# Attention with hash buckets and a routed expert: products with 128 rows, 16-byte places for V, signs as bits and complements

## The chip, the core and the metric

The kernel runs on one core of one Trainium2 chip, in one launch. The metric is the time of one execution in microseconds. Three runs of the kernel before took 401.94, 402.27 and 403.64 us; the median is 402.27 us.

## The reference, cut to what matters

```python
# q, k, v: (B=4, H=8, S=768, D=64) float32; proj: (64, 6)
bits(x)  = (x @ proj > 0)                       # 6 bits per token
mask     = bucket(q)[:, None] == bucket(k)[None, :]
scores   = where(mask, q @ k.T / 8, -1e9);  scores -= max(scores)
attn     = exp(scores) / (sum + 1e-9);      x = attn @ v      # 32 heads
# then, per batch b, x is (768, 512):
s        = x @ w_gate;  top = the 128 tokens with the largest s
out      = x;  out[top] += sigmoid(s[top]) * (relu(x[top] @ w1) @ w2)
```

## The kernel before, in words

The 32 heads go through one software pipeline. For each head there are two tiles in SBUF of 16-bit numbers. Tile A (97 partitions) holds q and k, split to their high parts, in rows 32 to 95, and sign rows for the hash above them: rows 0 to 5 are the centred signs of q and k (plus or minus 2^13), and row 6 is a constant row (2^13 for q, -6 * 2^13 for k), so that a product over these rows is 0 where all six signs agree and very negative elsewhere. Row 96 has -2^12 on k's side and, on q's side, the row's maximum divided by 2^12, which a later step puts there. Tile B (128 partitions) holds the low parts that correct the product. The region of A between q and k (tile K) has the difference of k's two halves.

Four kinds of product fill TensorE. `max_unit` (line 645) multiplies rows 0 to 95 of A, 384 columns at a time, twice for each of six row blocks: once with the difference of the halves, once with the second half. ScalarE takes the positive part of the one (`max_relu`, line 653), VectorE adds the other and keeps the maximum (`max_red`, line 662). When all six maxima of a head are there, TensorE turns them (`max_turn`), ScalarE copies them (`max_copy`), and SyncE's queue sends them as a row into A (`max_row`). `st_unit` then forms the scores minus the maximum, transposed: a product with 97 rows of A (line 693) and one with 128 rows of B (line 697) into the same PSUM bank, with 512 or 256 columns. ScalarE takes the exponential (`st_exp`, lines 711 and 713); VectorE or GpSimd splits it into a 16-bit high part, which is read in place, and a low part R (`r_chunk`, lines 728 and 731). `av` (line 755) multiplies these with V, in groups of three for each block of 128 by 128: high part with V's high part (65 columns: 64 and the sum), high part with V's low part (64 columns), low part with V's high part (65 columns). Each call of `av` does three such groups. `recip` and `norm` divide.

V sits in SBUF as [128, 6 blocks, 2 heads, 131 numbers of 2 bytes]: one number for the gate's score, 64 of V's high part, one for the sum, then the low part. Thirty-one heads skip the first number, so the high part that is read starts 2 bytes, and the low part 134 bytes, behind a multiple of 262 bytes.

Signs of all heads but the first come from `hash_half` (fp32 products, line 472) and `signs` (lines 489 to 496, VectorE): compare with zero, subtract the halves, subtract 2^13. Two DMAs for each head place them (`place_signs`). The first head has steps of its own at the start: `init_first` loads q and k, `hash_first` hashes them, `sign_first` (line 402) and `centre_first` (line 414) make the signs, `diff_first` (line 420) the difference. `init_crow` and `init_a` write the constant row with GpSimd, and `init_row` row 96. `keep_warm` issues products of ones that nobody reads.

The order of all this is written out by hand: `ORDER` lists 2698 steps, and each engine's queue, SyncE's DMAs too, gets its instructions in that order. Nothing is reordered after that.

Of the kernel before, what the change touches and what calls it, by code (L numbers as in the profile page):

```python
# [20 lines left out]
P = 128  # L21
NC = S // P
# [6 lines left out]
SG = 2.0 ** 13  # L29
MS = 2.0 ** 12  # L30
# [5 lines left out]
VC = 2 * D + 3  # L36
# [13 lines left out]
PJW = 66  # L50
ORDER = (
# [189 lines left out]
def body(ctx, tc, qk, v, pj, wg, w1, w2, cst, out):  # L241
# [348 lines left out]
    def sum_v(pr):  # L590
# [5 lines left out]
        if not o0:  # L596
            need("gvl")
# [730 lines left out]
```

## Time and profile before

| | |
|---|---|
| median of three runs | 402.27 us |
| profiled execution | 401.58 us |
| its span, first to last instruction | 399.8 us |
| TensorE busy | 387.0 us, 97% of the span |
| VectorE busy | 336.9 us, 84% |
| ScalarE busy | 332.8 us, 83% |
| GpSimd busy | 184.5 us, 46% |
| mean granted TensorE clock | 0.995 |

The prediction is worked out against the profiled execution, which spent 1.8 us outside its span. A product on TensorE overlaps the next one, so the duration of one in a row is longer than its share of the engine; what one product costs is read from the start of one row to the start of the next. `PE` is TensorE, `PEld` its loads of the stationary operand, `DVE` VectorE, `ACT` ScalarE, `POOL` GpSimd.

### The profile page before, as it was taken

The numbers are of one execution on the slowest core, as the hardware profiler recorded it, in microseconds if no ns is written. First come the engines' busy times: TensorE is split into PE (matmuls) and PEld (weight loads), VectorE is DVE, ScalarE is ACT, GpSimd is POOL, SyncE is SP. The second block draws the span as 40 slices with busy tenths as digits, with TensorE's granted clock in tenths as the row PEclk, the third lists the DMA queues.
The fourth block names the chain that finished last, engine by engine and source line by source line (L and its number), as shares of the span: only waits on it lengthen the run. The fifth ranks groups of instructions, "written<-read, shape, count | busy, mean of one in ns | idle before, by whom it ended". The sixth has DMA issues, their size and how long they took to land.

```text
span 399.8 us, 14395 instructions
## 1 busy us (share of the span) xinstructions
PE 387.0 (97%) x5770; PEld 278.3 (70%) x5770; DVE 336.9 (84%) x929; ACT 332.8 (83%) x818; POOL 184.5 (46%) x107
## 2 busy tenths in 40 slices
PE   5899999999999998999999999999999999999995
PEld 4356677677667776678567777677677778687794
DVE  4989898889999988987999798989999979769733
ACT  6779999999999998997769999999898997775310
POOL 7526576665756446345233444363525270520112
PEclk9989999999999999999999999999999999999999
DMA  6558655766665555546265636565163526100211
GB/s 221 134 164 233 191 157 170 212 163 175 186 222 132 146 177 154 173 118 181 74 184 161 147 91 172 154 200 171 42 162 93 139 44 170 24 21 2 105 32 53
DMA packets 25619, 55.44 MB, mean 139 GB/s; under 512 B 3850, under 2 KB 10582, under 8 KB 25552
## 3 DMA queue, kind: packets, MB, share of 16 engines
q1 hardware_dynamic: 15104, 35.97, 34.5%
q10 hardware_dynamic: 9680, 16.45, 12.5%
q0 software_dynamic: 768, 2.11, 1.7%
q8 instruction: 45, 0.74, 0.8%
q14 instruction: 22, 0.18, 0.2%
HBM read 26.19 MB, written 7.35 MB: 84 GB/s over the span
## 4 chain that ended last, share of the span: by engine, by line
PE 83%; issue 9%; DMA 2%; POOL 2%; ACT 2%; DVE 1%; POOLq 0%; SPq 0%; DVEq 0%; ACTq 0%
PE av L755 24%; PE st L693 15%; PE bank L645 15%; PE st L697 15%; PE bank L472 3%; PE bank L973 3%; PE bank L997 2%; DMA A<-mr 2%; PE av L740 1%; PE wq L303 1%; PE bank L601 1%; DMA Xa<-in_qk_dram 1%; ACT me L653 1%; POOL R L731 1%; DVE R L728 1%
## 5 line engine op out<-in xcount | busy, mean ns | idle before, releaser
L731 POOL TENSOR_TENSOR R<-P 128x1536 f16<-128x1536 f32 x46 | 135.9, 2957 | 153.4 <-ACT P L711 31.9
L755 PEld LDWEIGHTS <-P 128*128 128x128 bf16 x2304 | 129.0, 97 | 29.1 <-issue 1.0
L755 PE MATMUL av<-V,P 128*128 128x65 f16 (+2 forms) x2304 | 136.9, 194 | 0.0
L755 PE MATMUL av<-V,R 128*128 128x65 f16 (+1 forms) x1152 | 129.6, 193 | 0.8 <-DVE R L728 0.8
L711 ACT ACTIVATE P<-st 128x512 f32<-128x512 f32 x192 | 113.9, 608 | 14.9 <-PE st L697 8.9
L693 PE MATMUL st<-A 97*128 97x256 f16 (+1 forms) x384 | 120.7, 329 | 0.7 <-DMA A<-mr 0.5
L662 DVE CUSTOM_DVE_ANT_0 mj<-bank,me 128x384 bf16<-128x384 f32 x192 | 102.4, 553 | 21.6 <-ACT me L653 9.4
L697 PE MATMUL st<-B 128*128 128x256 f16 (+1 forms) x384 | 120.5, 328 | 0.0
L645 PE MATMUL bank<-A 96*128 96x384 f16 x384 | 107.6, 327 | 1.8 <-DVE M L662 0.7
L755 PEld LDWEIGHTS <-R 128*128 128x128 f16 x1152 | 107.5, 99 | 1.0 <-DVE R L728 1.0
L653 ACT ACTIVATE me<-bank 128x384 f32<-128x384 f32 x192 | 93.8, 503 | 12.2 <-PE bank L645 5.6
L728 DVE TENSOR_TENSOR R<-P 128x768 f16<-128x768 f32 x100 | 94.6, 966 | 1.2 <-ACT P L713 1.0
L713 ACT ACTIVATE P<-st 128x512 f32<-128x512 f32 x96 | 58.1, 609 | 1.3 <-PE st L697 1.3
L693 PEld LDWEIGHTS <-A 97*128 97x128 f16 x384 | 37.7, 98 | 17.4 <-issue 2.6
L697 PEld LDWEIGHTS <-B 128*128 128x128 f16 x384 | 37.8, 99 | 15.2 <-issue 0.9
L645 PEld LDWEIGHTS <-A 96*128 96x128 f16 x384 | 34.7, 98 | 19.2 <-issue 2.7
L779 ACT ACTIVATE x<-av,rc 128x64 f32<-128x64 f32 x192 | 44.1, 331 | 0.5 <-DVE rc L767 0.4
L509 DVE SCALAR_TENSOR_TENSOR T<-X,T 128x768 f16<-128x768 f32 x32 | 35.2, 1102 | 0.5 <-ACT T L502 0.5
L502 ACT ACTIVATE T<-X 128x768 f16<-128x768 f32 x32 | 27.1, 857 | 0.0
L973 PEld LDWEIGHTS <-w1h 128*128 128x128 f16 x256 | 15.8, 98 | 1.9
L816 POOL TENSOR_TENSOR w1l<-W,w1h 128x512 bf16<-128x512 f32 x8 | 12.2, 1522 | 10.0 <-ACT P L711 3.9
L662 DVE DVE_READ_ACCUMULATOR2_ANT M<- 128x1 f16 x192 | 16.4, 86 | 0.0
(138 smaller groups left out, 409.2 us busy)
## 6 DMA issues: line engine op xcount, KB each, us to landing
X<-in_qk_dram SPq DMA_DIRECT2D x32, 384.0 KB
B<-T SPq DMA_DIRECT2D x62, 192.0 KB
A<-T SPq DMA_DIRECT2D x31, 240.0 KB
V<-in_v_dram ACTq DMA_DIRECT2D x16, 384.0 KB
out_dram<-x ACTq DMA_DIRECT2D x6, 768.0 KB
W<-in_w_dram ACTq DMA_DIRECT2D x8, 512.0 KB
sbc<-scores SPq DMA_DIRECT2D x3, 384.0 KB
out_3l_dram<-x ACTq DMA_DIRECT2D x1, 768.0 KB
```

The costliest lines, as they stand in the source:

```text
L509: mine(nc.vector.scalar_tensor_tensor(t[:, o : o + S], st["X", p, r], XS, t[:, i : i + S], op0=ALU.mult, op1=ALU.subtract))
L645: nc.tensor.matmul(pt[:, :384], a[0][0:96, t * P : (t + 1) * P], a[1][0:96, 384:768] if i else K[h % NA][0:96], start=True, stop=True,)
L653: nc.scalar.activation(me, st["mx", h, t, 0][:, :384], AF.Relu)
L662: nc.vector.tensor_tensor_reduce(out=jk, in0=st["mx", h, t, 1][:, :384], in1=st["me", h, t], op0=ALU.add, op1=ALU.max, scale=1.0 / MS, sca ...
L693: nc.tensor.matmul(pt[:, o : o + n], a[1][:, c * P : (c + 1) * P], a[0][:, q0 : q0 + n], start=True, stop=False,)
L697: nc.tensor.matmul(pt[:, o : o + n], bt[:, 0, c * P : (c + 1) * P], bt[:, 1, q0 : q0 + n], start=False, stop=True,)
L711: nc.scalar.activation(pp[:, r, 0:512], pt, AF.Exp, scale=ES)
L713: nc.scalar.activation(pp[:, :, 512:768], pt.rearrange("p (a b) -> p a b", a=2), AF.Exp, scale=ES)
L728: mine(nc.vector.tensor_tensor(t[:, r], pp[:, r], hi_view(pp, r), op=ALU.subtract))
L731: turn(nc.gpsimd.tensor_tensor(t, pp, hi_view(pp, a), op=ALU.subtract))
L755: nc.tensor.matmul(o[:, t, o0:o1], l, vv[:, c, hh, v0 + o0 : v0 + o1], start=False, stop=last and l is lo, skip_group_check=True,)
L779: nc.scalar.activation(x[:, t], o[:, t, 1 : D + 1], AF.Copy, scale=rc[:, t : t + 1])
```

## The change

Four parts.

First, tile A has 128 partitions, and the products of lines 645 and 693 read all of them. GpSimd zeroes rows 96 to 127 at the start (and rows 0 to 31 for three of the four tiles), in `init_a`. The maximum's row moves among the sign rows.

Second, the signs are 0 or a constant, not plus or minus: each of the six bits has a row, and so has its complement, for which the projection is written a second time and `negate` (ScalarE, once) turns it. The compare of `signs` and `sign_first` takes its threshold and its factor from a table with one value for each partition. In that table two further rows come out as constants: the one that was row 6, and the one in which the maximum is put later, which is 0 on q's side until then. So 14 rows are placed for each head, where it was 6, by the same two DMAs. Centring goes: the last instruction of `signs` (line 496), `centre_first`, `init_crow`, `init_row` and the DMAs of the constant row.

Third, V has 144 numbers in the place of 131: V's high part and the sum from 0, the gate's score behind them, the low part from 72. High and low part then start at multiples of 16 bytes. The output columns in PSUM start at 0, no longer at 1.

Fourth, `ORDER` is another list of 2692 steps. Of the steps that both have, half moved by at most 8 places and one in ten by more than 20. At the start, two of the `keep_warm` steps (34 and 8 products) and `negate` stand ahead of `hash_first`; before, 34 stood behind it.

```diff
-VC = 2 * D + 3
+VL = 72
+VC = 2 * VL
-PJW = 66
+PJW = 68
+PF = 27
+QC, KC = 2 * SG, -SG * NB
 ORDER = (
...
-        t = cp.tile([97, KH + S - QH], F16, name=f"A{i}")
+        t = cp.tile([P, KH + S - QH], F16, name=f"A{i}")
...
     def init_a(i):
         st["ia", i] = True
-        e = nc.gpsimd
-        e.memset(AA[i][0:32].bitcast(F32), 0.0)
-        e.dma_start(AA[i][6:7], crow)
+        for p in (0, 96) if i else (96,):
+            nc.gpsimd.memset(AA[i][p : p + 32].bitcast(F32), 0.0)
...
+    def negate():
+        n = 2 * NB + 2
+        x = pjt[:, NB : NB + 3 * n].rearrange("p (j t) -> p j t", t=n)[:, :, :NB]
+        nc.scalar.activation(x, x, AF.Copy, scale=-1.0)
...
         nc.vector.tensor_scalar(
-            sg[:, e * 384 : (e + 1) * 384], hp[r, :384], 0.0, 2 * SG,
+            sg[:, e * 384 : (e + 1) * 384], hp[r, :384], pjt[r, 66:67], pjt[r, 67:68],
             op0=ALU.is_gt, op1=ALU.mult,
         )
         if e:
             nc.vector.tensor_tensor(sd, sg[:, 0:384], sg[:, 384:768], op=ALU.subtract)
-            nc.vector.tensor_scalar(sg, sg, SG, None, op0=ALU.subtract)
...
-        move(a[0:6, KD - QH :], t[j + 32 : j + 38])
-        move(a[0:6, 0:S], t[j : j + 6, S // 2 :])
+        move(a[0:n, KD - QH :], t[j + 32 : j + 32 + n])
+        move(a[0:n, 0:S], t[j : j + n, S // 2 :])
...
         nc.tensor.matmul(
-            pt[:, :384], a[0][0:96, t * P : (t + 1) * P],
-            a[1][0:96, 384:768] if i else K[h % NA][0:96], start=True, stop=True,
+            pt[:, :384], a[0][:, t * P : (t + 1) * P],
+            a[1][:, 384:768] if i else K[h % NA], start=True, stop=True,
         )
...
-        move(A[h % NA][0][96:97], st["mr", h])
+        r = 1 if (h - 1) % 2 else 2 * NB + 1
+        move(A[h % NA][0][r : r + 1], st["mr", h])
...
-        o, o0 = st["O", h], int(h < NH - 1)
+        o, (e, f) = st["O", h], ((OW, OW) if h == NH - 1 else (D + 1, D))
...
-            for l, o1, v0 in ((hi, OW, 0), (hi, D + 1, OW), (lo, OW, 0)):
+            for l, n, v0 in ((hi, e, 0), (hi, f, VL), (lo, e, 0)):
                 nc.tensor.matmul(
-                    o[:, t, o0:o1], l, vv[:, c, hh, v0 + o0 : v0 + o1], start=False,
+                    o[:, t, :n], l, vv[:, c, hh, v0 : v0 + n], start=False,
                     stop=last and l is lo, skip_group_check=True,
                 )
```

## Rows read from the trace of the kernel before

**Rows 1.** The page: busy us of an engine (share of the span), instructions.

```profile
PE 387.0 (97%) x5770; PEld 278.3 (70%) x5770; DVE 336.9 (84%) x929; ACT 332.8 (83%) x818; POOL 184.5 (46%) x107
```

**Rows 2.** Stretches: us, each engine's busy us, PEclk, DMA share, GB/s.

```profile
10.00:20.00 10.00, 8.12 (x55) 3.22 (x52) 9.12 (x25) 7.06 (x13) 5.93 (x18) 1.00 0.54 134
20.00:30.00 10.00, 9.88 (x83) 5.52 (x83) 8.19 (x23) 7.81 (x19) 2.96 (x2) 0.83 0.58 165
30.00:60.00 30.00, 30.00 (x449) 21.15 (x447) 27.12 (x74) 30.00 (x74) 19.69 (x10) 1.00 0.67 193
60.00:100.00 40.00, 40.00 (x623) 28.30 (x622) 35.24 (x94) 39.22 (x102) 24.50 (x11) 1.00 0.64 180
100.00:140.00 40.00, 39.93 (x620) 28.22 (x619) 37.76 (x105) 38.36 (x98) 22.69 (x10) 1.00 0.62 171
...
200.00:240.00 40.00, 40.00 (x659) 28.84 (x658) 35.81 (x105) 35.39 (x91) 16.71 (x7) 1.00 0.54 146
```

**Rows 3.** TensorE's timeline, 192 to 195 us: start, us, line, tiles, shape, count.

```profile
192.22 0.38 PE L997 MATMUL bank<-w2h,hth 128*128 128x512 f16 x1
...
194.16 0.65 PE L645 MATMUL bank<-A 96*128 96x384 f16 x3
```

**Rows 4.** The chain of waits, 66 to 69 us: start, us, what.

```profile
66.26 0.11 PE st L693
...
68.30 0.22 PE st L697
68.52 0.83 PE av L755 x27
```

**Rows 5.** TensorE's timeline, 186 to 188 us.

```profile
186.45 0.22 PE L755 MATMUL av<-V,P 128*128 128x65 f16 x2
...
187.80 0.20 PE L755 MATMUL av<-V,R 128*128 128x65 f16 x1
187.84 0.33 PE L645 MATMUL bank<-A 96*128 96x384 f16 x1
```

**Rows 6.** TensorE's timeline, 262 to 263 us.

```profile
262.43 0.22 PE L755 MATMUL av<-V,P 128*128 128x65 f16 x2
...
262.94 0.19 PE L755 MATMUL av<-V,R 128*128 128x65 f16 x1
262.97 0.22 PE L672 MATMUL bank<-ident,M 128*128 128x128 f16 x1
```

**Rows 7.** TensorE's groups by line and shape: count, busy us, mean ns.

```profile
L755 PE MATMUL av<-V,P 128*128 128x65 f16 x1152 | 129.7, 193 | 0.0
...
L693 PE MATMUL st<-A 97*128 97x512 f16 x192 | 73.6, 383 | 0.5 <-DMA A<-mr 0.5
```

**Rows 8.** All engines' timeline, 0 to 13 us.

```profile
0.75 0.20 POOL L292 MEMSET ones<- 128x128 f16 x1 [0.29 <-POOLq L1308]
...
4.26 1.51 PE L393 MATMUL bank<-Xa,pjt 96*32 96x384 f32 x8 [4.26 <-DMA Xa<-in_qk_dram]
...
5.70 3.81 PE L303 MATMUL wq<-ones 128*128 128x128 f16 x34
...
5.93 1.70 DVE L402 TENSOR_SCALAR A<-bank 7x384 f16<-7x384 f32 x3 [3.42 <-PE bank L393]
...
11.48 1.23 PE L645 MATMUL bank<-A 96*128 96x384 f16 x5
...
12.97 0.56 DVE L662 CUSTOM_DVE_ANT_0 mj<-bank,me 128x384 bf16<-128x384 f32 x1
```

**Rows 9.** VectorE's groups by line: count, busy us, mean ns, idle before.

```profile
L496 DVE TENSOR_SCALAR sg<-sg 128x768 f16<-128x768 f16 (+1 forms) x9 | 3.9, 429 | 0.3
...
L414 DVE TENSOR_SCALAR A<-A,pjt 7x384 f16<-7x384 f16 (+1 forms) x3 | 0.9, 333 | 0.0
```

**Rows 10.** The chain of waits, 140 to 268 us.

```profile
148.61 3.13 DMA A<-mr
...
263.51 2.91 DMA A<-mr
```

More of the change, by code (lines that the diff above doesn't have):

```diff
@@ L29 @@
 SG = 2.0 ** 13
+TH = -(2.0 ** -126)
 MS = 2.0 ** 12
@@ L270, in body @@
     AA, A, Bt, V, K = [], [], [], [], []
-    crow = sb.tile([1, KH + S - QH], F16, tag="x", name="crow", bufs=1)
     for i in range(NA):
-        t = cp.tile([97, KH + S - QH], F16, name=f"A{i}")
+        t = cp.tile([P, KH + S - QH], F16, name=f"A{i}")
         AA.append(t)
@@ L306, in keep_warm @@
         heat(pst.tile([P, 512], F32, tag="st", name=f"wq{i}"), n)
-    def init_row(i):
-        nc.gpsimd.memset(A[i][1][96:97], -MS)
-    def init_crow():
-        for c, a, b in ((SG, 0, S), (0.0, S, KH - QH), (-SG * NB, KH - QH, KH - QH + S)):
-            nc.gpsimd.memset(crow[:, a:b], c)
     def init_a(i):
         st["ia", i] = True
-        e = nc.gpsimd
-        e.memset(AA[i][0:32].bitcast(F32), 0.0)
-        e.dma_start(AA[i][6:7], crow)
+        for p in (0, 96) if i else (96,):
+            nc.gpsimd.memset(AA[i][p : p + 32].bitcast(F32), 0.0)
     def init_rest():
@@ L329, in init_rest @@
         for t in V:
-            nc.gpsimd.memset(t[:, :, :, D + 1 : OW], VS)
-        for x in (0, OW):
-            nc.gpsimd.memset(V[-1][:, :, 0, x : x + 1], 0.0)
+            nc.gpsimd.memset(t[:, :, :, D : D + 1], VS)
+        for x in (D + 1, VL + D, VL + D + 1):
+            nc.gpsimd.memset(V[-1][:, :, :, x : x + 1], 0.0)
     w1h = cp.tile([P, 4, FF], F16, name="w1h")
@@ L393, in hash_first @@
                 nc.tensor.matmul(
-                    hp[j : j + 32, :384], pjt[0:96, 32:64], st["xa"][0:96, r, e * 384 : (e + 1) * 384],
+                    hp[j : j + 32, :384], pjt[0:96, PF : PF + 32], st["xa"][0:96, r, e * 384 : (e + 1) * 384],
                     start=True, stop=True, tile_position=(0, j),
@@ L400, in sign_first @@
         need(("xa", r))
-        j = 32 * (2 * e + r)
+        j, n = 32 * (2 * e + r), 2 * NB + 2
         nc.vector.tensor_scalar(
-            A[0][r][0:7, e * 384 : (e + 1) * 384], st["hpa"][j : j + 7, :384], 0.0, 2 * SG,
-            op0=ALU.is_gt, op1=ALU.mult,
+            A[0][r][0:n, e * 384 : (e + 1) * 384], st["hpa"][j : j + n, :384],
+            pjt[j : j + n, 64:65], pjt[j : j + n, 65:66], op0=ALU.is_gt, op1=ALU.mult,
         )
@@ L408, in sign_first @@
             pmax.give("hpa")
-    def centre_first(r, e):
-        f = slice(0, S) if e is None else slice(e * 384, e * 384 + 384)
-        need(*(("sa", r, x) for x in ((0, 1) if e is None else (e,))))
-        a = A[0][r][0:7, f]
-        nc.vector.tensor_scalar(a, a, pjt[0:7, 64 + r : 65 + r], None, op0=ALU.subtract)
-        st["ca", r, e] = True
     def diff_first():
-        need(("ca", 1, None))
+        need(("sa", 1, 0), ("sa", 1, 1))
         st["ia", 0] = True
@@ L430, in low_first @@
     def low_first(r):
-        need(("xs", r))
-        if r:
-            need(("ca", 1, None))
-        else:
-            need(("ca", 0, 0), ("ca", 0, 1))
+        need(("xs", r), ("sa", r, 0), ("sa", r, 1))
         if "xla" not in st:
@@ L461, in row_first @@
             )
-        nc.scalar.copy(A[0][0][96:97, e * 384 : (e + 1) * 384], pt[96:97, :384])
+        nc.scalar.copy(A[0][0][0:1, e * 384 : (e + 1) * 384], pt[0:1, :384])
         pmax.give(f"mt0_{e}")
@@ L518, in place_signs @@
     def place_signs(h):
-        p, j = (h - 1) // 2, 64 * ((h - 1) // 2 % 2) + 6 * ((h - 1) % 2)
+        n = 2 * NB + 2
+        p, j = (h - 1) // 2, 64 * ((h - 1) // 2 % 2) + 2 * NB * ((h - 1) % 2)
         need(("sgd", p, 0), ("sgd", p, 1))
@@ L555, in split_vh @@
         st["vh", pr] = True
-        nc.scalar.activation(V[pr % NV][:, :, :, 1 : D + 1], st["V", pr], AF.Copy, scale=VS)
+        nc.scalar.activation(V[pr % NV][:, :, :, :D], st["V", pr], AF.Copy, scale=VS)
     def split_vl(pr):
@@ L562, in split_vl @@
         nc.vector.scalar_tensor_tensor(
-            vv[:, :, OW + 1 :], t.rearrange("p c h d -> p (c h) d"), VS, vv[:, :, 1 : D + 1],
+            vv[:, :, VL : VL + D], t.rearrange("p c h d -> p (c h) d"), VS, vv[:, :, :D],
             op0=ALU.mult, op1=ALU.subtract,
@@ L578, in score_vh @@
     def score_vh():
-        nc.scalar.activation(V[-1][:, :, 1, 0:1], st["gv"], AF.Copy, scale=VS)
+        nc.scalar.activation(V[-1][:, :, 1, D + 1 : OW], st["gv"], AF.Copy, scale=VS)
         st["gvh"] = True
@@ L584, in score_vl @@
         nc.vector.scalar_tensor_tensor(
-            V[-1][:, :, 1, OW : OW + 1], st["gv"], VS, V[-1][:, :, 1, 0:1],
+            V[-1][:, :, 1, VL + D + 1 : VL + OW], st["gv"], VS, V[-1][:, :, 1, D + 1 : OW],
             op0=ALU.mult, op1=ALU.subtract,
@@ L594, in sum_v @@
         o, vv = sp[:, : 2 * OW].rearrange("p (h d) -> p h d", h=2), V[pr % NV]
-        o0 = int(pr < NH // 2 - 1)
-        if not o0:
+        last = pr == NH // 2 - 1
+        if last:
             need("gvl")
+        e, f = (OW, OW) if last else (D + 1, D)
         for i in range(2 * NC):
             c, j = i % NC, 32 * (i % 4)
-            v = vv[:, c, :, o0:OW] if i < NC else vv[:, c, :, OW + o0 :]
+            v = vv[:, c, :, :e] if i < NC else vv[:, c, :, VL : VL + f]
             nc.tensor.matmul(
-                o[j : j + 32, :, o0 : OW if i < NC else D + 1], tiny16, v,
+                o[j : j + 32, :, : e if i < NC else f], tiny16, v,
                 start=(i < 4), stop=(i >= 2 * NC - 4), tile_position=(0, j), skip_group_check=True,
@@ L607, in sum_hi @@
     def sum_hi(pr):
-        o0 = int(pr < NH // 2 - 1)
+        e = OW if pr == NH // 2 - 1 else D + 1
         st["wh", pr] = True
-        nc.scalar.copy(WH[:, :, o0:OW], st["sp", pr][:, :, o0:OW])
+        nc.scalar.copy(WH[:, :, :e], st["sp", pr][:, :, :e])
     def sum_lo(pr):
@@ L616, in sum_lo @@
         st["wl", pr] = True
-        o0 = int(pr < NH // 2 - 1)
+        e = OW if pr == NH // 2 - 1 else D + 1
         nc.vector.scalar_tensor_tensor(
-            W[pr % 2][:, :, o0:OW], WH[:, :, o0:OW], cs[:, 3 * P + 2 * NC :],
-            st["sp", pr][:, :, o0:OW], op0=ALU.mult, op1=ALU.subtract,
+            W[pr % 2][:, :, :e], WH[:, :, :e], cs[:, 3 * P + 2 * NC :],
+            st["sp", pr][:, :, :e], op0=ALU.mult, op1=ALU.subtract,
         )
@@ L659, in max_red @@
         if ("m", h) not in st:
-            st["m", h] = M[h % 2] if h else M[0][:, 96:]
+            st["m", h] = M[h % 2]
         jk = sb.tile([P, 384], BF16, tag="jks", name=f"mj{h}_{t}", bufs=2)
@@ L762, in recip @@
         need(*(("avs", h, i) for i in range(0, 36, 3)))
-        s = st["O", h][:, :, D + 1 : OW]
+        s = st["O", h][:, :, D : D + 1]
         rc = sb.tile([P, NC], F32, tag="rc", name=f"rc{h}", bufs=2)
@@ L778, in norm @@
         for t in range(3 * e, 3 * e + 3):
-            nc.scalar.activation(x[:, t], o[:, t, 1 : D + 1], AF.Copy, scale=rc[:, t : t + 1])
+            nc.scalar.activation(x[:, t], o[:, t, :D], AF.Copy, scale=rc[:, t : t + 1])
     def score(b, part, d0, d1, t0, t1):
@@ L1112, in rank_last @@
         nc.vector.tensor_tensor(
-            sc.unsqueeze(2), st["O", NH - 1][:, :, 0:1], st["rc", NH - 1].unsqueeze(2), op=ALU.mult
+            sc.unsqueeze(2), st["O", NH - 1][:, :, D + 1 : OW], st["rc", NH - 1].unsqueeze(2), op=ALU.mult
         )
@@ L1198, in body @@
     for fn in (
-        init_first, init_m, init_crow, load_consts, make_ident, make_consts, load_gate, init_rest,
-        hash_first, diff_first,
+        init_first, init_m, load_consts, make_ident, make_consts, load_gate, init_rest,
+        negate, hash_first, diff_first,
     ):
@@ L1203, in body @@
     for i in range(NA):
-        at(init_row, i)
-        if i:
-            at(init_a, i)
+        at(init_a, i)
     for r in range(2):
@@ L1211, in body @@
             at(sign_first, r, e)
-    for a in ((1, None), (0, 0), (0, 1)):
-        at(centre_first, *a)
     for i, n in enumerate(WARM):
@@ L1296 @@
     pj = np.zeros((P, PJW), f)
-    pj[32 : 32 + D, 32 : 32 + NB] = proj
-    pj[:NB, 64:66] = SG
-    pj[NB, 64:66] = -SG, SG * NB
-    pj[:D, 0:NB] = proj
-    pj[D:, NB : 2 * NB] = proj
+    n = 2 * NB + 2
+    for j in (0, NB):
+        pj[:D, j : j + NB] = proj
+        pj[D:, n + j : n + j + NB] = proj
+        pj[32 : 32 + D, PF + 1 + j : PF + 1 + j + NB] = proj
+    tab = np.zeros((2, 32, 4), f)
+    tab[0, :, 1::2], tab[1, :, 1::2] = SG, 2 * SG
+    for r, (c, z) in enumerate(((QC, 0.0), (KC, -MS))):
+        tab[r, 1 + NB : 1 + 2 * NB, 0] = TH
+        for j in (NB, n + NB):
+            tab[r, j : j + NB, 2] = TH
+        for j, t, x in ((0, 0, z), (n - 1, 0, c), (n - 2, 2, c), (n - 1, 2, z)):
+            tab[r, j, t : t + 2] = -1.0, x
+    pj[:, 64:68] = np.concatenate([tab, tab]).reshape(P, 4)
     wg = np.ascontiguousarray(np.broadcast_to(moe_w_gate[None, :], (P, DM)))
```

312 rows, old and new, of the table ORDER are left out of this document.

## Prediction

> **What bounds the kernel now.** I read the page first. TensorE is busy 387.0 of 399.8 us, and the next two engines 83 to 84% [rows 1]. So what a product costs TensorE is the first question; what the others allow is the second. For the second I read busy time by stretches: from 30 to 240 us TensorE has no gap worth naming (40.00 of 40), but ScalarE is full too in the first part of it: 30.00 of 30, 39.22 of 40 and 38.36 of 40 us, that is 107.6 of 110 us between 30 and 140. Later it is not: 35.39 of 40 between 200 and 240 [rows 2]. The reader should keep both facts: TensorE time saved late is saved; saved between 30 and 140 us it meets a ScalarE with 2.4 us left. The start is a third regime: from 10 to 20 us TensorE is busy 8.12 us, VectorE 9.12 of 10, and in the next 10 us TensorE's granted clock is 0.83 on the mean, so for a part of it it stood at 1.2 of 2.4 GHz [rows 2].
>
> Then I compared starts on TensorE. Nine products of 512 columns and 128 rows, one behind the other, take 194.16 - 192.22 = 1.94 us [rows 3]. Their columns at 2.4 GHz take 9 x 213.3 = 1.920 us, so one costs its columns plus 2.2 ns. That is the yardstick.
>
> **128 rows.** Between 66.26 and 68.52 us there are 15 products of lines 693, 697 and 645 in a chain without a gap: eight of 256 columns, four of 512, three of 384, in all 5248 columns [rows 4]. By the yardstick they take 2.187 + 15 x 0.0022 = 2.220 us; they take 2.26. Lines 693 and 697 alternate between 97 and 128 rows and line 645 has 96; among the 15 there are 14 at which the number of rows differs from that of the product before (two of line 645 follow each other). 0.040 us over 14 is 2.9 ns for each change of rows (the rows' last digit makes it 2.2 to 3.6). In the whole trace, the neighbours on TensorE with 128 stationary columns and 16-bit numbers change their rows 1160 times: 384 times from line 693 to 697, the rest where 693 or 645 begin or end. With 128 rows everywhere none is left. The term is 1160 x 2.9 = 3.4 us, bounded by 0 and 4.2.
>
> The Trainium skill ("TensorE: Matmul & The Clock Gate", "Part 2: What happens when you issue a matmul") says that the number of rows doesn't matter to the time of a product or of a load. By that the term would be 0. No row shows 97 rows dearer than 128 by themselves; what costs is the change, of which the page says nothing.
>
> **V at multiples of 16 bytes.** The 45 products of line 755 between 186.45 and 187.84 us are 15 groups of three in 1.39 us, 92.7 ns each [rows 5]. By the yardstick (65 + 64 + 65 columns, three times 2.2 ns) a group takes 87.4: 5.3 ns are lost, although nothing changes its rows. With the layout of before, V's low part starts at 262 (2c + h) + 134 bytes, a multiple of 16 for c = 3 in odd heads alone. Six such groups stand between 262.43 and 262.97 us: 0.54 us, 90.0 ns each, 2.6 lost [rows 6]. So an aligned low part gives back half. An aligned high part alone (c = 2 in odd heads) shows no gain in the trace, and the two together are not in it. There are 1152 groups [rows 7]. From both sides: 0, if those rows mislead, and 1152 x 5.3 = 6.1 us, if both parts together remove the whole stall. I take 2.0 ns for a group, a little under the nearest rows' 2.7, since few groups bear them: 2.3 us.
>
> The sum on TensorE is 5.7 us. Some 30% of the products lie between 30 and 140 us. Of their 1.7 us I count 0.7, because ScalarE's queue is full there and the same exponentials must pass; of the other 4.0 I count 3.8. Together 4.5, bounds 1 and 9.5.
>
> **Signs.** VectorE loses nine instructions of line 496, 3.9 us, and three of line 414, 0.9 us [rows 9]. From 30 us on VectorE is not what TensorE waits for, so eight of the nine are worth nothing; the cover is TensorE's own work. The compare keeps its size. Each head's two sign DMAs carry 14 rows where there were 6, on the same queue and at the same places: nothing, while the transfer engines are at 0.46 to 0.67 [rows 2]. `negate` is one short ScalarE instruction ahead of the first hash.
>
> **The start.** Before, the first hash starts at 4.26 us, when its data land, and takes 1.51 us; then VectorE makes signs (1.70 us for three), centres them and subtracts; the first product of line 645 comes at 11.48, the first maximum at 12.97 us [rows 8]. The 34 products of ones run meanwhile, 3.81 us, 0.11 each. In the new order 42 of them stand ahead of the hash. The ones are written by 0.95 us, so the hash starts at about 0.95 + 42 x 0.11 = 5.6 us, 1.3 us later than its data, and ends at 7.1. Three signs make 8.8, a subtraction of some 0.3 makes 9.1: the first product of line 645 comes some 2 us earlier than before. VectorE then still has four sign instructions to do before its first maximum, at about 11.5 us, 1.5 us earlier. I count 1.5 us, as ScalarE, which is full from 30 us on, starts earlier too. Bounds: -0.5 (the later hash is all that counts) and 3 (the stretch at the low clock goes as well).
>
> **The order.** Its waits can't be read from rows of before. The two visible ones there are the maxima's row on its way, 3.13 us at 148.61 and 2.91 us at 263.51 [rows 10], with gaps of TensorE behind them. I assume as many in the new order: 0.
>
> **The sum.** 4.5 + 1.5 = 6.0 us: 401.58 - 6.0 = 395.6 us for a profiled execution. That execution is 0.7 us under the median, so I predict 396.3 us; with the bounds of the terms 391 to 400.
>
> **Rivals.**
> (a) V's stall stays whole. For: the aligned groups are few. Against: [rows 6]. Then 5.7 falls to 3.4 us and the sum to 4.2: 398.1 us.
> (b) V's stall goes whole, since both parts are aligned. For: half goes with one. Against: the high part alone shows nothing. Then TensorE saves 9.5 us, the sum is 8.6: 393.7 us.
> (c) The rows don't matter, and what I priced is the change of the product's line. Against: pairs of line 645 in a row go without it, and so do the expert's products, which change operands. By this, as a mechanism here, 3.4 us don't come: 399.0 us. It is the skill's rule above.
> (d) ScalarE sets the pace nearly everywhere, and the start gives nothing. For: [rows 2], 30 to 140 us. Against: 35.39 of 40 later. Then some 1 us is left: 401.3 us.
> (e) Slower: the new order sends the maxima's row too late. Its way takes 2.9 to 3.1 us [rows 10]. Counting TensorE's work in the list between `max_row` and the first product of line 693 that reads it, by the prices above, the old order has one head of 31 under 0.9 us; the new one has nine at 0.6 us or less, two of them at 0.2 and one at 0. The list is not time, other engines run behind it, so a short distance need not stall. If these nine heads wait 1.2 us each, 10.8 us come on top of -6.0: 407.1 us. It decides from 8 us of such waits on; with less the change is still no slower.
>
> **Chances.** Forecast 0.42 (393 to 399.5), (a) 0.15, (b) 0.15, (c) 0.05, (d) 0.12, (e) 0.11. A measurement of this kernel tells 0.5% from no change, 400.3 to 404.3 us. Below lie the forecast, (a), (b), (c) and a little of (d): 0.79. Within: most of (d), 0.10. Above: (e), 0.11. The range that leaves out two in ten goes from 391 (rival b with the good bound of the start) to 402.5.
>
> **What would show it.** Rows right: pairs of lines 693 and 697 start 431 ns apart for 512 columns, not 436 to 438, and line 755's first product behind line 645 costs as much as its others. V right: a group takes about 90 ns (87.4 for rival b, 92.7 for a). Start right: first product of line 645 before 9.5 us, first maximum before 12. ScalarE as a bound: its busy share from 30 to 140 us stays at 98% or more while TensorE gets gaps there. The prediction is wrong in its main step if TensorE's distances shrink as said and the time does not, or if gaps of TensorE behind the maxima's row come to more than 3 us in all.

## The result and the profile after

The changed kernel takes 396.9 us, median of four runs (395.7 to 397.8); the kernel before took 402.1 us beside it. The ratio is 0.987, 95% interval 0.982 to 0.992. The forecast was 396.3 us. The profiled execution took 397.28 us, its span is 395.2 us.

First the page of the kernel after, its busy times, as in [rows 1]:

```profile
PE 381.3 (96%) x5762; PEld 275.7 (70%) x5770; DVE 337.1 (85%) x917; ACT 330.4 (84%) x819; POOL 185.0 (47%) x102
```

TensorE's busy time fell by 5.7 us with nearly as many instructions, VectorE's not at all, although twelve instructions are gone. The stretches of [rows 2], after (us, busy us of PE, PEld, DVE, ACT, POOL, then PEclk, DMA share, GB/s):

```profile
10.00:20.00 10.00, 6.94 (x39) 2.45 (x38) 9.73 (x25) 7.00 (x14) 6.46 (x18) 1.00 0.49 136
20.00:30.00 10.00, 9.28 (x109) 6.17 (x110) 8.80 (x25) 8.77 (x21) 4.36 (x2) 1.00 0.83 227
30.00:60.00 30.00, 29.87 (x439) 20.18 (x436) 26.82 (x72) 29.78 (x77) 17.21 (x7) 1.00 0.68 188
60.00:100.00 40.00, 39.84 (x633) 28.42 (x632) 35.81 (x92) 39.26 (x102) 25.54 (x11) 1.00 0.61 171
100.00:140.00 40.00, 40.00 (x630) 28.73 (x627) 37.24 (x111) 38.97 (x98) 22.89 (x10) 1.00 0.66 197
200.00:240.00 40.00, 39.89 (x655) 28.70 (x651) 34.63 (x105) 37.10 (x96) 18.17 (x7) 1.00 0.52 134
```

The reader is to see two things. From 30 to 140 us ScalarE is busy 108.0 of 110 us (it was 107.6), and TensorE, which had been full there, has a little air. And the stretch at a granted clock of 0.83 after 20 us is gone.

The rows answer directly. In the chain of waits of the kernel after (start, us, what) 17 products of scores and maxima stand between 291.81 and 294.36 us: eight of 256 columns, four of 512, five of 384, in all 6016.

```profile
291.81 0.11 PE st L684
291.92 0.11 PE st L688
...
294.03 0.33 PE bank L635 x2
294.36 0.11 PE bank L855
```

They take 2.55 us; the yardstick of [rows 3] gives 2.507 + 17 x 0.0022 = 2.54. The few nanoseconds that [rows 4] showed on top are gone. Over all pairs of the scores' two products with one after the other, the median distance of starts is 216 ns for 512 columns (219 before) and 109 for 256 (112 before).

For V, TensorE's timeline of the kernel after (start, us, line, tiles, shape, count), six groups of three, as in [rows 5]:

```profile
186.56 0.23 PE L746 MATMUL av<-V,P 128*128 128x65 f16 x2
...
187.07 0.20 PE L746 MATMUL av<-V,R 128*128 128x65 f16 x1
187.10 0.38 PE L988 MATMUL bank<-w2h,hth 128*128 128x512 f16 x1
```

0.54 us for six groups is 90.0 ns each, where [rows 5] had 92.7. A call of nine products (three groups) takes 269.9 ns in the mean of 363 calls, 276.7 before.

The start, to be held against [rows 8]:

```profile
1.01 4.66 PE L306 MATMUL wq<-ones 128*128 128x128 f16 x42 [1.01 <-POOL ones L295]
5.60 1.19 PE L393 MATMUL bank<-Xa,pjt 96*32 96x384 f32 x8
6.93 2.08 DVE L402 TENSOR_SCALAR A<-bank,pjt 14x384 f16<-14x384 f32 x3 [4.43 <-PE bank L393]
9.16 3.42 POOL L427 TENSOR_TENSOR XLa<-Xa,A 96x768 f16<-96x768 f32 x2 [3.09 <-DVE A L402]
9.46 0.32 PE L635 MATMUL bank<-A 128*128 128x384 f16 x1 [1.03 <-DVE A L413]
11.54 1.25 DVE L484 TENSOR_TENSOR sg<-sg 64x384 f16<-64x384 f16 x1
12.99 0.54 DVE L652 CUSTOM_DVE_ANT_0 mj<-bank,me 128x384 bf16<-128x384 f32 x1
```

The hash starts at 5.60 us, as worked out, and the first product of the maxima comes 2 us earlier than before. But the first maximum comes at 12.99 us, and it had been 12.97. VectorE stands between the two: three compares take 2.08 us where they took 1.70. Its groups of compares (count, busy us, mean ns), first before, then after:

```profile
L489 DVE TENSOR_SCALAR sg<-bank 128x384 f16<-128x384 f32 (+1 forms) x18 | 9.8, 554 | 2.2 <-PE bank L472 1.9
L402 DVE TENSOR_SCALAR A<-bank 7x384 f16<-7x384 f32 x4 | 2.2, 551 | 3.5 <-PE bank L393 3.4
```

```profile
L478 DVE TENSOR_SCALAR sg<-bank,pjt 128x384 f16<-128x384 f32 (+1 forms) x18 | 11.8, 676 | 0.5 <-PE bank L461 0.3
L402 DVE TENSOR_SCALAR A<-bank,pjt 14x384 f16<-14x384 f32 x4 | 2.7, 672 | 4.5 <-PE bank L393 4.4
```

22 compares became 0.12 us longer each: 2.6 us. So more than half of what [rows 9] gave back, 4.8 us, is spent again.

### The profile page after: what moved, and what is told of

Same layout as the page of the kernel before. It is cut to its first block, busy times and chain, and to the rows that moved or that the text cites. A ratio compares the mean times of both kernels' runs of the same rounds, so it can differ in the third digit from the quotient of the medians.

```text
span 395.2 us, 14356 instructions
## 1 busy us (share of the span) xinstructions
PE 381.3 (96%) x5762; PEld 275.7 (70%) x5770; DVE 337.1 (85%) x917; ACT 330.4 (84%) x819; POOL 185.0 (47%) x102
## 4 chain that ended last, share of the span: by engine, by line
PE 78%; DVE 7%; issue 5%; ACT 3%; POOL 3%; DMA 3%; POOLq 0%; SPq 0%; ACTq 0%; DVEq 0%
PE av L746 23%; PE st L684 15%; PE st L688 14%; PE bank L635 14%; PE bank L964 2%; PE bank L461 2%; PE bank L988 2%; DMA A<-mr 2%; DVE R L719 2%; PE av L731 2%; PE wq L306 1%; ACT x L770 1%; DVE mj L652 1%; DMA B<-XLa 1%; PE bank L591 1%
## 5 line engine op out<-in xcount | busy, mean ns | idle before, releaser
L746 PEld LDWEIGHTS <-P 128*128 128x128 bf16 x2304 | 126.0, 98 | 27.3 <-issue 0.8
L746 PE MATMUL av<-V,P 128*128 128x65 f16 (+2 forms) x2304 | 133.3, 193 | 0.1
L746 PE MATMUL av<-V,R 128*128 128x65 f16 (+1 forms) x1152 | 126.5, 193 | 1.2 <-DVE R L719 1.2
L702 ACT ACTIVATE P<-st 128x512 f32<-128x512 f32 x192 | 114.6, 620 | 11.5 <-PE st L688 8.2
L684 PE MATMUL st<-A 128*128 128x256 f16 (+1 forms) x384 | 119.2, 326 | 1.0 <-DMA A<-mr 0.7
L688 PE MATMUL st<-B 128*128 128x256 f16 (+1 forms) x384 | 118.7, 326 | 1.1 <-DMA B<-XLa 1.1
L635 PE MATMUL bank<-A 128*128 128x384 f16 x384 | 107.6, 326 | 3.3 <-DVE M L652 1.2
L746 PEld LDWEIGHTS <-R 128*128 128x128 f16 x1152 | 105.8, 97 | 1.3 <-DVE R L719 1.3
L719 DVE TENSOR_TENSOR R<-P 128x768 f16<-128x768 f32 x100 | 96.8, 988 | 5.9 <-ACT P L704 5.5
L635 PEld LDWEIGHTS <-A 128*128 128x128 f16 x384 | 34.7, 97 | 23.0 <-issue 7.6
L684 PEld LDWEIGHTS <-A 128*128 128x128 f16 x384 | 37.4, 97 | 15.0 <-issue 0.9
L497 DVE SCALAR_TENSOR_TENSOR T<-X,T 128x768 f16<-128x768 f32 x32 | 31.6, 999 | 0.0
```

The costliest lines, as they stand in the source:

```text
L497: mine(nc.vector.scalar_tensor_tensor(t[:, o : o + S], st["X", p, r], XS, t[:, i : i + S], op0=ALU.mult, op1=ALU.subtract))
L635: nc.tensor.matmul(pt[:, :384], a[0][:, t * P : (t + 1) * P], a[1][:, 384:768] if i else K[h % NA], start=True, stop=True,)
L684: nc.tensor.matmul(pt[:, o : o + n], a[1][:, c * P : (c + 1) * P], a[0][:, q0 : q0 + n], start=True, stop=False,)
L688: nc.tensor.matmul(pt[:, o : o + n], bt[:, 0, c * P : (c + 1) * P], bt[:, 1, q0 : q0 + n], start=False, stop=True,)
L702: nc.scalar.activation(pp[:, r, 0:512], pt, AF.Exp, scale=ES)
L719: mine(nc.vector.tensor_tensor(t[:, r], pp[:, r], hi_view(pp, r), op=ALU.subtract))
```

## The experiments

**Undoing the two TensorE parts, one by one and together.** First the changed kernel itself, as a control on the same chip.

> The changed kernel itself, on the same chip and in the same rounds as the three kernels below, so that each is compared with it by its ratio to the kernel before. Its profile said 397.3 us against 401.6, a ratio of 0.987. All theories: 0.985 to 0.989.

Measured: 396.2 us, ratio 0.988 (0.984 to 0.991).

```diff
-            pt[:, :384], a[0][:, t * P : (t + 1) * P],
-            a[1][:, 384:768] if i else K[h % NA], ...
+            pt[:, :384], a[0][0:96, t * P : (t + 1) * P],
+            a[1][0:96, 384:768] if i else K[h % NA][0:96], ...
...
-                pt[:, o : o + n], a[1][:, c * P : (c + 1) * P], a[0][:, q0 : q0 + n],
+                pt[:, o : o + n], a[1][0:97, c * P : (c + 1) * P], a[0][0:97, q0 : q0 + n],
```

> The changed kernel with 96 rows in the maxima's products and 97 and 128 in turn in the scores', as before; the rows left out are zeros, so the result stays. My theory: each of the 1160 changes of rows between neighbours costs TensorE 2 to 3 ns, so 512-column products of the scores start 218 to 219 ns apart and not 216, the mean call of nine products on V stays at 270 ns, TensorE works 3.4 us more, and the time rises by 2.3 to 3.4 us against the changed kernel (399.2 to 400.3). Rival (rows don't matter, what I priced was something else that the change brought): distances stay at 216 ns and the time within 0.5 us of the changed kernel. Second rival (TensorE's gain was eaten, so it was worth nothing): distances grow as in my theory, the time does not.

Measured: 399.6 us, ratio 0.994 (0.992 to 0.997). The chain of this kernel over the same 17 products:

```profile
293.74 0.11 PE st L684
293.85 0.11 PE st L688
...
296.00 0.33 PE bank L635 x2
296.32 0.11 PE bank L855
```

2.58 us and not 2.55; the median distance of 512 columns is 219 ns again, of 256 columns 112. The distances are as I said, and the rival by which the rows don't matter falls.

Rows back and the control issue the same products in the same order, so their two traces can be laid side by side, product by product (16-bit, 128 stationary columns, waits left out). The 1113 products that stand right behind a change of rows take 2.8 ns longer in rows back, 3.1 us in all. The other 4032 take 0.75 us less in all; why is open. TensorE so pays about 2.3 us net, not 3.4. The time is no clean measure of this: of the twelve runs, the seven with a mean granted clock of 0.987 or less take 399.4 to 401.7 us and the other five 397.0 to 400.1. That the median lies in the range I gave is luck in part.

```diff
-VL = 72
-VC = 2 * VL
+VL = 67
+VC = 133
```

> The changed kernel with V's two parts at odd places again (67 elements from the high to the low part, 133 for a head and chunk); among them two chunks of odd heads have an aligned low part alone, and two chunks of even heads an aligned high part alone. My theory: a call of nine products on V goes from 270 back to 276 or 277 ns, 384 calls make 2.3 to 2.7 us on TensorE and 1.6 to 2.4 us in time; the chunks with the low part aligned stay near 271, those with the high part alone show no relief. Rival (the shorter low part, 64 columns in place of 65, or another difference made the calls shorter): calls stay at 270 ns, time within 0.5 us of the changed kernel.

Measured: 398.3 us, ratio 0.992 (0.989 to 0.995). A call takes 275.8 ns in the mean. It tells more than that, since the places differ by chunk. Two calls of head 17 in its timeline, the first with the low part at a multiple of 16 bytes and the second with neither part so:

```profile
214.28 0.22 PE L746 MATMUL av<-V,P 128*128 128x65 f16 x2
...
214.55 0.23 PE L746 MATMUL av<-V,P 128*128 128x65 f16 x2
...
214.83 0.22 PE L746 MATMUL av<-V,P 128*128 128x65 f16 x2
```

0.27 and 0.28 us. Over the whole trace: chunks whose low part alone is aligned take 270.3 and 271.4 ns a call (30 and 29 calls), those whose high part alone is aligned 275.7 and 276.1 (32 and 32), the others 275 to 280. The next kernel has the same places and gives the same means within 0.3 ns. The changed kernel with both aligned takes 269.9. So the low part alone gives nearly all of it. The change also moved the output columns in PSUM by one, which this kernel doesn't undo; the 0.9 ns between its 275.8 and the 276.7 of before are all that can be due to it.

> The changed kernel with both of these undone; what is left of the change are the signs and the order. My theory: the two costs add, 4.4 to 5.8 us over the changed kernel, so 401.3 to 402.7 us, a ratio of 0.998 to 1.002 to the kernel before: signs and order together are worth nothing, where the prediction had given the start 1.5 us. Rival (the start did give its 1.5 us and a part of TensorE's gain was lost instead): 399 to 400.5 us.

Its edit is both of the above. Measured: 401.1 us, ratio 0.998 (0.996 to 1.001). Signs and order together are worth 0.6 us, between 1.6 and -0.3, as in my theory; what each of them is worth alone was not run.

The four traces say where the gain went. For each kernel I add up, over all 16-bit neighbours on TensorE with 128 stationary columns, how much the distance of their starts exceeds the columns at 2.4 GHz plus 2.1 ns, where it is at most 15 ns (more is a wait). The stretches end where head 0's and head 11's products on V begin, and with the last product:

| kernel | to head 0, us | losses to head 11 | its length | losses to the end | its length |
|---|---|---|---|---|---|
| before | 28.63 | 3.18 | 115.15 | 6.19 | 250.74 |
| changed (control) | 27.51 | 1.47 | 113.83 | 2.97 | 248.19 |
| rows back | 28.34 | 2.32 | 114.46 | 4.38 | 249.91 |
| V back | 28.06 | 2.10 | 114.20 | 4.17 | 249.11 |
| both back | 28.27 | 3.08 | 114.85 | 5.77 | 251.03 |

Both parts together save TensorE 1.61 us in the middle stretch, where ScalarE is full, and the time there falls by 1.02. In the last stretch they save 2.80 us, and against the control the time falls by 2.84. This last number doesn't compare like with like. The profile after is of the same kernel as the control; its middle stretch agrees with the control's (113.84 us), but its last takes 249.26, 1.07 more. With it goes how a GpSimd and a VectorE subtraction meet near 151 us, here in the profile after and then in the control:

```profile
150.65 1.15 POOL L807 TENSOR_TENSOR w2l<-W,w2h 128x512 bf16<-128x512 f32 x1
150.89 1.73 DVE L719 TENSOR_TENSOR R<-P 128x768 f16<-128x768 f32 x1
```

```profile
150.74 0.97 DVE L719 TENSOR_TENSOR R<-P 128x768 f16<-128x768 f32 x1
150.86 1.88 POOL L807 TENSOR_TENSOR w2l<-W,w2h 128x512 bf16<-128x512 f32 x1
```

The one that begins first keeps its time. Where that is GpSimd's, TensorE waits 1.6 us between 140 and 205 us; where it is R, 0.9 us. The other profiles with the same work on TensorE fall alike: their last stretch takes 248.2 to 248.5 us where R begins first (control, its repeat, start-sp) and 249.1 to 249.3 where GpSimd's does (the profile after, the kernel with constants). In rows back and both back GpSimd's begins first, as in the profile after. Against that profile the last stretch falls by 1.77 of 2.80 us, a share of 0.63, the same as in the middle.

The first column is something else (below); because of it the medians of these kernels scatter by a us or two (rows back from 397.0 to 401.7 us, the changed kernel from 395.8 to 397.7). The stretches measure the two parts better than the medians do, if the meeting falls the same way in both.

**Is it the change of rows, or 97 rows?**

```diff
+                pt[:, o : o + n], bt[0:97, 0, c * P : (c + 1) * P], bt[0:97, 1, q0 : q0 + n],
```

(and 97 rows in the other products of scores and maxima)

> The changed kernel with 97 rows in all products of scores and maxima; it leaves out rows 97 to 127 of the scores' second product (a part of the low-order sums). No row change is left inside a pair of scores, nor between scores and maxima; some 700 remain where these meet products of 128 rows on V and in the expert. Read from the trace alone, the time of one run says little. Theory A (the change of rows between neighbours costs): pairs of 512 columns start 216 ns apart, as with 128 rows. Theory B (97 rows are dearer than 128, whatever the neighbour has): pairs start 218 to 219 ns apart or more, as in the kernel before.

The chain over the same 17 products:

```profile
291.72 0.11 PE st L684
291.83 0.11 PE st L688
...
293.94 0.33 PE bank L635 x2
294.27 0.11 PE bank L855
```

2.55 us, and 216 ns is the median distance for 512 columns. Theory A: 97 rows are as cheap as 128; the change costs. In this trace 476 changes are left, not some 700, and side by side with the control the 451 products behind one (waits left out) take 3.1 ns longer. One run, 397.3 us.

**A coarser place for V.** The edit: `VL = 96`.

> The changed kernel with V's parts 96 elements apart (high parts at multiples of 128 bytes, low parts of 64 bytes) instead of 72. A call of nine products on V takes 270 ns in the changed kernel, its columns and the yardstick 262. Theory A (the stall left over is a matter of alignment too): the call falls to 262 to 266 ns and the time by 1 to 2.5 us. Theory B (what the 16 bytes gave is all, the rest comes from somewhere else): the call stays at 269 to 271 ns and the time within 0.5 us of the changed kernel's 396.2.

Measured: 396.9 us, ratio 0.988 (0.985 to 0.991); 269.5 ns a call. Theory B. What is left of the stall, some 8 ns a call over the yardstick, is not a matter of these places; its cause is open.

**What the longer compare costs.**

```diff
-            pjt[j : j + n, 64:65], pjt[j : j + n, 65:66], op0=ALU.is_gt, op1=ALU.mult,
+            0.0, 1.0, op0=ALU.is_gt, op1=ALU.mult,
...
-            sg[:, e * 384 : (e + 1) * 384], hp[r, :384], pjt[r, 66:67], pjt[r, 67:68],
+            sg[:, e * 384 : (e + 1) * 384], hp[r, :384], 0.0, 1.0,
```

> The changed kernel whose 22 sign compares take two constants instead of two columns of the table (what is left out: the table's constants, so complements, the two constant rows and the masks' size). Measured so far: the compare takes 0.67 us with the table against 0.55 us before. My theory: with constants it takes 0.55 us again, VectorE has 2.6 us less to do, the first maximum starts 0.4 to 0.6 us earlier (four or five compares stand ahead of it), and the time falls by 0.3 to 0.8 us against the changed kernel's 396.2, since later compares lie under TensorE's work. Rival (VectorE sets the pace in many places): the time falls by 1.5 to 2.6 us. Second rival (the two columns are not what makes it longer, the 14 rows or the 64 rows at other places are): compares stay at 0.67 us and nothing changes.

Its groups of compares:

```profile
L478 DVE TENSOR_SCALAR sg<-bank 128x384 f16<-128x384 f32 (+1 forms) x18 | 9.9, 555 | 1.9 <-PE bank L461 1.5
L402 DVE TENSOR_SCALAR A<-bank 14x384 f16<-14x384 f32 x4 | 2.2, 551 | 3.3 <-PE bank L393 3.2
```

So the two columns of the table cost the 0.12 us, not the 14 rows. The first maximum comes at 12.31 us, where the control has 13.17. The time is 397.9 us, ratio 0.990 (0.987 to 0.993): no gain that can be told. That fits VectorE's 2.6 us lying under TensorE's work, but doesn't show it. My 0.3 to 0.8 us were not confirmed.

**The start.** Its first candidate, fewer ones:

```diff
-WARM = (34, 8, 8, 8, 6, 6)
+WARM = (24, 6, 8, 8, 6, 6)
```

and `negate` ahead of `split_first`.

> The changed kernel with 30 products of ones ahead of the first hash instead of 42, and the sign change of the projection ahead of the first split on ScalarE. My theory (VectorE's chain from the hash on sets the start): ones end at 1.0 + 30 x 0.11 = 4.3 us, the hash starts there and not at 5.6, the first product of the maxima at 8.2 to 8.6 us instead of 9.46, the first maximum near 12 instead of 12.99; the time falls by 0.6 to 1.2 us. Rival (the clock): with fewer ones the granted clock rises later, the hash takes 1.5 us instead of 1.2 and a stretch at the low clock comes back at 20 us: the time stays or rises by up to 1 us. Second rival (a later wait takes its place, the place of the low part of the first head at 19.3 to 20.7 us): the time stays within 0.3 us.

A miss: 401.2 us, ratio 0.996 (0.992 to 0.999). The twelve runs lie in two groups, five from 396.7 to 398.6 us and seven from 401.1 to 402.1; the profiled one is of the upper group. TensorE's timeline (this and the next three kernels have their lines 155 lower):

```profile
1.01 3.38 PE L151 MATMUL wq<-ones 128*128 128x128 f16 x30 [1.01 <-POOL ones L140]
4.32 1.51 PE L238 MATMUL bank<-Xa,pjt 96*32 96x384 f32 x8
8.67 2.77 PE L306 MATMUL bank<-X,pjt 128*32 128x384 f32 x8 [2.84 <-DMA X<-in_qk_dram]
11.38 1.88 PE L480 MATMUL bank<-A 128*128 128x384 f16 x5
```

The first hash starts at 4.32 as planned. Then TensorE stands 2.84 us for the second hash's input X, and the eight products that follow take 2.77 us; they take 1.48 in the changed kernel. Rows back has a like wait, 2.97 us, and the same 2.77 us behind it, and there the profile shows a granted clock of 0.50, the lower of the two levels, 1.2 GHz, from 8 to 18 us. In the trace of this kernel the row reads 1.00 at that place, so it doesn't show why the products are slow there; it shows 0.50 later, after a second wait, one of 2.0 us at 24 us. One stretch of rows back and two of this kernel:

```profile
16.00:18.00 2.00, 2.00 (x7) 0.32 (x6) 1.83 (x7) 1.03 (x2) 1.76 (x4) 0.50 0.39 83
```

```profile
10.00:12.00 2.00, 2.00 (x9) 0.42 (x6) 1.69 (x3) 0.08 (x1) 0.26 (x1) 1.00 0.07 27
28.00:30.00 2.00, 2.00 (x9) 1.06 (x7) 1.41 (x4) 1.81 (x5) 0.26 (x1) 0.50 0.24 39
```

So a stretch at the low clock comes back, as the clock rival said, and the hash takes 1.51 us; but the stretch follows a wait of TensorE, and whether the number of ones has a part in it is not shown. Nor does each such wait end so: with constants in the compare TensorE waited 2.52 us for X, its clock stayed at 1.00 and the eight products took 1.48 us. What the wait at 24 us is for, and two more at 82 and 112 us, the trace doesn't say: open.

This pointed to X. In the profiled executions of kernels with the same start it landed anywhere from 6.66 to 9.12 us. Two of them, V at 96 and rows back:

```profile
6.66 1.48 PE L461 MATMUL bank<-X,pjt 128*32 128x384 f32 x8 [0.96 <-DMA X<-in_qk_dram]
```

```profile
8.92 2.77 PE L461 MATMUL bank<-X,pjt 128*32 128x384 f32 x8 [2.97 <-DMA X<-in_qk_dram]
```

Products on V of head 0 began at 25.9 and 28.3 us there. So the first column of the table above scatters by 2 us whatever is changed. The three latest, 28.1 to 28.3 us, had X late and the clock at 0.50 behind it. But X is not all: in the profile after it landed at 6.94 us, and head 0 began at 27.29.

A second wait in the changed kernel was for the first head's operand B:

```profile
20.72 0.38 PE L688 MATMUL st<-B 128*128 128x512 f16 x1 [1.09 <-DMA B<-XLa]
```

> The changed kernel with the three transfers of the first head's operand B, and the low part's subtraction, moved ahead of the second head's operand A in the queue. After the change the first product on B waits 1.09 us at 19.3 to 20.7 us for the transfer B<-XLa. My theory: the transfer lands before 18 us, the first scores' pair runs without the gap, the first exponential starts about 1.1 us earlier (21.14 now), and the time falls by 0.7 to 1.2 us. Rival (the row of the first head's maxima at 19.2 us and VectorE set the start): the gap only moves to the next products, the time stays within 0.3 us. Second rival: the transfers for the second head (A<-T, A<-sg), now up to 1.5 us later, become a gap of TensorE before 30 us, and the time rises.

Measured: 396.3 us, ratio 0.985 (0.982 to 0.988). That gap is gone and head 0 begins at 26.23, but V at 96 began at 25.92 without this edit: not told apart from the changed kernel. Then both together, with the loads of heads 3 and 4 (`load_x(1, ...)`) behind `place_first(1)` in the list:

> The changed kernel with the loads X of heads 3 and 4 sent behind the first transfer B<-A, so that the loads of heads 1 and 2 have the transfer engines to themselves, and the transfers B<-A and B<-XLa of the first head sent as in the kernel with these moved up. In the profiled executions so far the second hash's input lands anywhere from 6.66 to 9.12 us, and TensorE's products on V of the first head start between 25.9 and 28.3 us accordingly. My theory (1.9 MB of loads share the engines until then): it lands before 6.8 us, the hash follows the first without a gap, products on V of the first head start at 25 to 26 us, and the time is 0.7 to 2 us under the changed kernel's 396.2, with less spread. Rival (VectorE's own work between 7 and 20 us sets the start whatever lands): products on V still start at 26 to 27.5 us and the time stays within 0.5 us. Second rival (what is sent later is then late: the second hash for heads 3 and 4 at 11.9 us): a gap comes there and the time rises.

Measured: 395.5 us, ratio 0.983 (0.979 to 0.988). X landed at 7.40 us, later than I said, and head 0 began at 25.16, 2.35 us before the control's. At the end 0.97 us were left of it. TensorE waits 1.2 us at 154 us, as the profile after does at 155 us; VectorE's and GpSimd's rows:

```profile
152.51 2.78 DVE L564 TENSOR_TENSOR R<-P 128x768 f16<-128x768 f32 x2
```

```profile
152.75 1.73 POOL L652 TENSOR_TENSOR w2l<-W,w2h 128x512 bf16<-128x512 f32 x1 [0.99 <-DVE T L342]
```

Two R take 2.78 us beside a subtraction of GpSimd. The last experiment puts that step (one entry of the list) behind the two:

> The kernel with the loads moved (start-x), and one subtraction on GpSimd (w2l) put behind VectorE's two subtractions R of head 12 instead of beside them. In start-x TensorE waits 1.2 us at 154 us for the second of these, which takes about 1.8 us beside GpSimd's where one alone takes 0.95. My theory (the two engines slow each other): both take 0.95 us each, the wait falls to 0.3 us or less, the start of the products on V of head 14 and all later ones come 0.6 to 1.1 us earlier than in start-x, time 394.4 to 395. Rival (ScalarE or the next wait sets the end there): the wait goes, the later starts stay within 0.3 us. Second rival (GpSimd's work, now later, slows the split of the next head): a gap of the same size comes behind it, time within 0.5 us.

```profile
151.55 1.81 DVE L564 TENSOR_TENSOR R<-P 128x768 f16<-128x768 f32 x2
```

> The changed kernel itself once more, on the same chip as the kernel with the moved loads and the moved subtraction, to compare the two in the same rounds. My theory: 1.2 to 2 us over it. Rival (the moved loads are worth less than one profiled run showed): within 0.7 us.

1.81 us for the two, the wait is gone, and all later heads come 1.4 us earlier than in start-x. Not all of this is the edit. In start-x GpSimd's began first at the earlier meeting too (148.80 against 149.15 us, R takes 1.61), so a part of its lost lead is the difference between the profile after and the control; in the last kernel R began first (148.81 against 148.92, 0.96 us), and the two R start 0.96 us earlier for it. Measured in the same rounds: 394.2 us, ratio 0.984 (0.982 to 0.986), against the changed kernel's 396.8 us, ratio 0.991 (0.989 to 0.994). This version beats both kernels. In the traces it is 2.75 us ahead of this run of the changed kernel, where R began first as well: 2.0 at the start and 0.7 later, about the 0.8 us that TensorE waits there for R. The ratios of start-x and of this version are the same, so the times don't show the subtraction's part. The Trainium skill ("SBUF — State Buffer", "Who interferes with whom") says that a VectorE instruction with two inputs in SBUF and a GpSimd instruction that reads SBUF exclude each other on a shared read interface, and the later one blocks. The trace agrees: one R takes 0.95 us alone, and the one behind GpSimd's start some 1.8.

## Why the prediction was right, step by step

**128 rows: right in mechanism and in the cost of a change, too large in the sum.** It said 1160 changes at 2.9 ns, 3.4 us. Side by side with the control, a product behind a change costs 2.8 ns. But TensorE's losses in rows back grow by (2.32 - 1.47) + (4.38 - 2.97) = 2.26 us only, as the products without a change lose less there; the prediction had no such term, and its cause is open. Rival (c), rows don't matter, is refuted by rows back, and rows-97 shows that the change is what counts.

**V: right, nearly to the number, for half a wrong reason.** It took 2.0 ns a group. The calls give (275.8 - 269.9) / 3 = 2.0 ns. But the prediction left open what both parts aligned would do. The answer is: about what the low part alone does. Rivals (a), no gain, and (b), the stall goes whole, both fall.

**TensorE's sum: 5.7 us said, 4.4 found** by both back, (3.08 - 1.47) + (5.77 - 2.97).

**What reaches the end: the split was wrong.** I counted 0.7 of 1.7 us between 30 and 140 us, since ScalarE is full there, and 3.8 of the later 4.0. Like with like, 1.02 of 1.61 came in the middle and 1.77 of 2.80 later. The share is 0.63 in both, so the traces don't bear out that a full ScalarE sets it, nor that what is saved late is all saved. 4.5 us were forecast and 2.8 measured in these stretches, from one profile each; with the control in the place of the profile after it would be 3.9. The ratios of control and both back, start included, differ by 1.06%, 4.3 us, which their intervals leave open by 1.7 us either way. Rival (d), ScalarE nearly everywhere with 1 us left, falls.

**Signs: a wrong step that cost little.** "The compare keeps its size" is wrong: 2.6 us more on VectorE. "Nothing" for the total of this part fits the run with constants all the same: without these 2.6 us no gain could be told.

**The start: 1.5 us were not there.** The first product of the maxima came at 9.46, as worked out, the first maximum at 12.99 and not at 11.5. Two terms were missed. The six compares ahead of it cost 0.7 us more; and the subtraction of line 484 takes 1.25 us beside GpSimd's of line 427, where line 495 took 0.35 before. Head 0 did begin 1.3 us earlier in the profile after, but profiles of kernels with this start have it anywhere between 25.9 and 28.3 us. Both back puts signs, start and order at 0.6 us (1.6 to -0.3).

**The order: no late row.** The maxima's row is on its way for 3.96 and 2.75 us, where [rows 10] has 3.13 and 2.91. The two waits, in the chain and on TensorE:

```profile
145.13 3.96 DMA A<-mr
...
259.58 2.75 DMA A<-mr
```

```profile
149.13 0.39 PE L684 MATMUL st<-A 128*128 128x512 f16 x1 [0.36 <-DMA A<-mr]
...
262.46 0.38 PE L684 MATMUL st<-A 128*128 128x512 f16 x1 [0.33 <-DMA A<-mr]
```

The gaps behind these two are 0.36 and 0.33 us and the only ones of their kind, far under the 3 us that were to show the main step wrong and the 8 us from which rival (e) would decide.

**The bounds.** The terms' own bounds, 1 to 9.5 and -0.5 to 3 us, add up to 389.8 to 401.8 us, a little wider than the 391 to 400 that stand there.

So the experiments give 2.8 + 0.6 = 3.4 us where the sum had 6.0 (4.5 with the control as the measure), and the medians before and after differ by 5.2 us (3.3 to 7.2 by the interval). The forecast came within 0.6 us with too much counted for TensorE's parts and 0.9 too much for the start. The closeness is luck in part: the scatter of the start and of the meeting near 151 us is as large as what was too much.

## What to carry to other kernels

Where TensorE is full, look at the distance of starts between neighbours, not at single durations: 2 to 3 ns at 2300 places are over 4 us here, and padding rows with zeros cost nothing on that engine. Don't count such a saving whole: 2.8 of 4.4 us reached the end. Before two profiles are subtracted, compare two profiles of one and the same kernel: here they differ by 1.07 us, and with it goes a tenth of a microsecond in which of two engines begins first. And before a step is put beside another at the start or elsewhere, look for what lands there and which two engines then run at once: start and subtraction together were worth 2.6 us in the same rounds.

## What the runs showed of the hardware

- On TensorE a product behind one with another number of stationary rows (96, 97 or 128) takes 2.8 ns longer in the mean of 1113 (512 columns: 219 ns to the next start, not 216); 97 rows behind 97 cost as much as 128 behind 128 (216 ns).
- V's low part at a multiple of 16 bytes makes a group of three products 2.0 ns shorter; the high part's place does nothing (275.7 ns a call as against 275 to 280), and multiples of 64 and 128 bytes give no more (269.5 as against 269.9).
- A compare on VectorE with two values for each partition takes 0.67 us, with two constants 0.55, on 384 columns.
- VectorE's R (two inputs in SBUF) takes 0.95 us alone. Where GpSimd's subtraction began 0.24 us ahead of it, R took 1.73 us and GpSimd's 1.15; where R began 0.12 us ahead, R took 0.97 and GpSimd's 1.88.
- In rows back TensorE stood still for 2.97 us for a late input; its granted clock was 0.50 from 8 to 18 us, and eight fp32 products took 2.77 us in the place of 1.48. After a wait of 2.52 us for the same input, in the kernel with constants, the clock stayed at 1.00.
